# Attention and a soft mixture of experts: TensorE's flips of x, logits and slot sums stand in the rounds that complete a query tile

## The chip, the core and the metric

The kernel runs on one core of a Trainium2 chip. The metric is the device time of one execution in microseconds (us), the median of several. The profile comes from one execution, taken by the hardware profiler. Its engines are TensorE (PE; PEld is its weight load), VectorE (DVE), ScalarE (ACT), GpSimd (POOL) and SyncE (SP), which issues nearly all transfers.

## The reference

```
scores = scale * q @ k^T                      # 8 batches, 8 heads, 576 x 576, head size 64
scores = where(0 <= i - j < 128, scores - slope_h * (i - j), -1e9)
attn   = softmax(scores) @ v
x      = attn, heads side by side: 4608 tokens x 512
logits = x @ phi                              # 32 slots: 8 experts x 4
d = softmax of logits over the 4608 tokens    # per slot
slot_input = d^T @ x
slot_out   = relu(slot_input @ w1[e]) @ w2[e] # per expert, hidden size 1024
c = softmax of logits over the 32 slots       # per token
out = c @ slot_out
```

## The kernel before

A query tile (b, t) is 128 queries of batch b (t = 0 to 3), or the last 64 (t = 4). It is done in groups (b, t, g) of four heads by 128 queries: two groups for t below 4, one for t = 4, 72 in all. The window of 128 keys lets a group look at its own tile's keys and those of the tile before.

The loop over `groups` (L777) emits one round for each group, and the order in which it emits is the order in which each engine runs, since the schedule is written out by hand (`manual_schedule`). Semaphores are set from what each step reads and writes, and a PSUM bank counts as one thing: two engines never use one bank at once. In round i:

- VectorE runs `softmax_front`: `merge` of group i (L286, puts masked keys right), `rowmax` (L300), `inverse` of group i-1 (L313), `bias` (L304), `normalise` of group i-1 (L317). Between them stand single steps of the slot softmax (`filler`).
- TensorE flips the probabilities of group i-3 (`flip`, L374), ScalarE copies the flip out (`split`, L380), and GpSimd makes from it the part that lies in the own tile and the part in the tile before (two selects, L386 and L388).
- TensorE runs `values` of group i-4 (L410): v times the probabilities, into the only buffer `xp`. Where that completes a tile, VectorE copies it into `x` (`x_store`, L424), and the next `values` waits for that copy.
- TensorE runs the scores of group i+1 (`scores`, L261 the bias, L270 the products), into one of two buffers, which the exponentials of group i-1 must have left.
- ScalarE runs the exponentials of group i (`expo`, L359).
- Last, TensorE's extra steps of that round run (`run("pe", i)`), and VectorE's (`run("dve", i)`). ScalarE's extra steps stand behind `split`, VectorE's of the kind "pre" at the head of the round.

For the rounds up to 6 the flip and `values` are one group further on, and round 7 (`SKIP`) has none of them.

The extra steps are those of the mixture. Tiles are gathered into passes of four (the eighth has three, the last two), each tile of a pass in a lane. `after_values` puts down, for each completed tile, in which round its steps run: `x_flip` (L438, TensorE, into the same two banks as the flip of the probabilities), and `x_keep` a round later (L447, ScalarE, into `xns`). For each completed pass it puts down a chain: `logits` (L456, TensorE, reads the four tiles in `xts`), `token_copy` (L464, ScalarE), `token_max` (L469, VectorE), `slot_flip` (L477, TensorE), `token_exp` (L484), `token_sum` (L496, VectorE), `token_flip` (L502, TensorE), `token_keep` (L507, ScalarE), `slots_max` (L536 and L537, VectorE), `slot_sum` (L514, TensorE, reads `xns`), `slots_exp` (L540), `slot_add` (L522, VectorE, scales and adds to `acc`), and `slots_norm` in three single steps (L547 to L549). `logits`, the flips and the slot sum all use one PSUM bank (tag "mi"), one after the other. `turn` and `ready` keep the order: an `x_flip` of a pass comes no earlier than the slot sum of the pass before, and no two are in one round.

`x_store` of a tile of pass k+1 overwrites the lane of `xts` (`x_of`, L416) in which the tile of pass k stood; the short tiles (t = 4) have a buffer of their own.

The transfers of q, k, v and the experts' weights are issued by SyncE in the order of emission, each when its buffer is free. After the rounds come the last pass, the slot inputs, the experts' two products and the output; that part is long and fully written out.

Of the kernel before, what the change touches and what calls it, by code (L numbers as in the profile page):

```python
# [44 lines left out]
LAG = 4  # L45
SKIP = 7
# [26 lines left out]
def tile_attn_softmoe(  # L73
# [60 lines left out]
    def load_weight():  # L134
        n = loaded[0]
        loaded[0] += 1
        m, e, k = units[n]
        if NW <= n < NW + len(place):
            wt[units[n]] = place[n - NW]
        else:  # L140
            wt[units[n]] = wpool.tile([P, UW], F32, tag="w", name=f"w{n}")
        nc.sync.dma_start(wt[units[n]], (w1d, w2d)[m][e, :, UW * k:UW * (k + 1)])
# [4 lines left out]
    def order(b):  # L147
        return (1, 2, 3, 4, 0) if b == last else range(NT)

    def pos(b, t):  # L150
        return order(b).index(t)
# [4 lines left out]
    end = len(passes) - 1  # L156
# [5 lines left out]
    groups = [(b, t, g) for b in range(B) for t in order(b) for g in range(2 if t < 4 else 1)]  # L162
    number = {key: i for i, key in enumerate(groups)}
    n = len(groups)
# [22 lines left out]
    def load_v(again=False):  # L187
        if again:
            b, t, v_slot[last, 0] = last, 0, area[:, 13]
        else:  # L190
            b, t = v_loads[len(v_taken)]
            v_slot[b, t] = vs[len(v_taken) % 3]
            v_taken.append((b, t))
        nc.sync.dma_start(v_slot[b, t][0:width(t)], vd[b, P * t:P * t + width(t)])

    def load_v_pair():
        new = [len(v_taken), len(v_taken) + 1]
        for i in new:
            v_slot[v_loads[i]] = vs[i % 3]
            v_taken.append(v_loads[i])  # L200
        for o in (0, DM // 2):
            for i in new:
                b, t = v_loads[i]
                nc.sync.dma_start(
                    v_slot[b, t][:, o:o + DM // 2], vd[b, P * t:P * t + P, o:o + DM // 2])
# [210 lines left out]
    def x_of(b, t):  # L416
        return xts[lane(b, t)] if t < 4 else xt_t

    def x_store(b, t, eng=None, js=slice(0, NPAIR)):
        src = st[b, t][:, js]  # L420
        o, w = (0, P) if t < 4 else (TAIL * (b % 2), TAIL)
        dst = x_of(b, t)[:, js, o:o + w]
        if eng is None:
            nc.vector.tensor_copy(dst, src[:, :, 0:w])  # L424
        else:
            eng.copy(dst, src[:, :, 0:w])
# [22 lines left out]
    def lanes(k):  # L449
        return len(passes[k])  # L450
# [253 lines left out]
    todo = {}  # L704

    def do(when, i, fn, *a):
        todo.setdefault((when, i), []).append((fn, a))
# [18 lines left out]
    def load_weights_at(i):  # L726
# [5 lines left out]
        if b == last and (t == 0 and g == 0 or t == 4):  # L732
            assert loaded[0] >= NW
            load_weight()

    def after_values(i, key):
        b, t, g = key
        if not (g == 1 or t == 4):
            return
        p = pos(b, t)  # L740
        if (b, p) == (last - 1, NT - 1):
            load_v_pair()
        elif b + p and len(v_taken) < len(v_loads):
            load_v()
        x_store(b, t)
        if (b, t) not in pass_of:
            return
        k, c = pass_of[b, t]
        turn[0] = max(i + 1, turn[0] + 1, ready.get(k - 1, 0) + 4)
        do("pe", turn[0], x_flip, b, t)  # L750
        if (b, t) != tiles[-1]:
            do("act", turn[0] + 1, x_keep, b, t)
        if c == lanes(k) - 1:
            ready[k] = i
            do("pe", i + 1, logits, k)
            if k == end:
                return
            assert turn[0] <= i + 3
            do("act", i + 2, token_copy, k)
            do("dve", i + 2, token_max, k)  # L760
            do("pe", i + 2, slot_flip, k)
            do("act", i + 3, token_exp, k)
            do("dve", i + 3, token_sum, k)
            do("pe", i + 3, token_flip, k)
            do("act", i + 4, token_keep, k)
            do("pre", i + 4, slots_max, k)
            do("pe", i + 4, slot_sum, k)
            do("act", i + 5, slots_exp, k)
            do("dve", i + 5, slot_add, k)
            do("dve", i + 6, later, slots_norm, k)  # L770

    turn, ready = [0], {}

    with tc.manual_schedule(engines=ORDERED):
        scores(0)
        loads(0)
        for i in range(n):  # L777
            new = groups[i]
            run("pre", i)
            if i:  # L780
                softmax_front(new, groups[i - 1])
            else:
                for us in (LO, HI):
                    merge(new, us)
                    rowmax(new, us)
                    bias(new, us)
                    expo(new, us)
            near = int(i < SKIP)
            if i + near >= FLAG and i != SKIP:
                flip(groups[i + near - FLAG])  # L790
                split(groups[i + near - FLAG])
            run("act", i)
            if i + near >= LAG and i != SKIP:
                values(groups[i + near - LAG])
                after_values(i, groups[i + near - LAG])
            if i + 1 < n:
                scores(i + 1)
            if i + 1 < n - 1:
                loads(i + 1)
            if i:  # L800
                expo(new)
            run("pe", i)
            load_weights_at(i)
            run("dve", i)
# [324 lines left out]
```

## Time and profile before

| | |
|---|---|
| median of 3 runs | 286.34 us (286.32 to 286.56) |
| the profiled execution | 286.09 us |
| its span | 284.3 us |
| mean granted TensorE clock | 0.992 |
| rounds | from about 5 to 212 us |
| transfers | 72.49 MB, mean 255 GB/s |

The busy times of the five engines over the span, the busy times of single stretches, the waits (who waited for whom: total, times, longest), the chain of work that ended last, and the timeline (start, duration, engine, line, operation) are the views that the text uses. A line such as `PE xp L410 <- DVE area L424` reads: TensorE, about to run line 410 that writes `xp`, stood idle until VectorE's line 424, which writes `area`, was done. `area` is one large tile in which `x`, the probabilities, v and their flips all lie.

### The profile page before, as it was taken

To read this page: it belongs to the slowest core of one execution; us is meant where nothing else is said; L and a number is where in the kernel's file an instruction comes from. 1 tells how busy PE (TensorE), PEld (TensorE's weight loads), DVE (VectorE), ACT (ScalarE), POOL (GpSimd) and SP (SyncE) were. 2 spreads that over 40 slices of the span, in tenths; PEclk is the share of its full clock that TensorE was granted. 3 is DMA by queue.
4 is the path that set the end of the run, shared out by engine and by line. 5 is a ranking of instruction groups with operands and counts; after the bars stand their busy time and mean duration, and the time that the engine had idled before them with its cause. 6 is when DMAs were issued, how large, how long until landed. Compare 5 with 4: busy or idle time off the path is not lost.

```text
span 284.3 us, 11675 instructions
## 1 busy us (share of the span) xinstructions
PE 257.5 (91%) x4575; PEld 180.7 (64%) x4575; DVE 218.6 (77%) x546; ACT 190.5 (67%) x780; POOL 111.7 (39%) x221
## 2 busy tenths in 40 slices
PE   7789898989899999998989998998989899999990
PEld 3567676767577677676667766766666443587750
DVE  1789998997998898899999899897973352656352
ACT  2868868887798887897897888887774411044460
POOL 3035734481574385265527526556452011000000
PEclk9999999999999999999999999999999999999996
DMA  5735368889786998889698778876565588999997
GB/s 167 238 110 153 115 173 250 255 247 295 252 277 184 303 303 262 257 265 285 221 298 283 255 236 280 268 212 218 166 213 199 172 257 296 417 416 373 376 357 295
DMA packets 36767, 72.49 MB, mean 255 GB/s; under 512 B 4413, under 2 KB 15337, under 8 KB 36713
## 3 DMA queue, kind: packets, MB, share of 16 engines
q1 hardware_dynamic: 35992, 71.25, 75.7%
q8 instruction: 36, 0.59, 0.8%
q10 hardware_dynamic: 720, 0.51, 0.6%
q14 instruction: 19, 0.15, 0.2%
HBM read 62.30 MB, written 9.44 MB: 252 GB/s over the span
## 4 chain that ended last, share of the span: by engine, by line
PE 44%; DVE 38%; ACT 9%; issue 3%; DMA 3%; POOL 1%; DVEq 0%; ACTq 0%; SPq 0%; POOLq 0%
DVE area L317 12%; DVE s L300 9%; PE xp L410 8%; ACT area L359 6%; PE op L967 5%; PE s L270 5%; DVE area L424 5%; PE hp L930 5%; DVE s L286 4%; PE po L992 4%; PE s L261 2%; PE lp L456 2%; PE pq L374 2%; DVE acc L522 2%; DMA area<-v_n 2%
## 5 line engine op out<-in xcount | busy, mean ns | idle before, releaser
L359 ACT ACTIVATE area<-s,nb 128x128 f32<-128x128 f32 x286 | 101.9, 379 | 21.6 <-DVE nb L304 20.2
L410 PE MATMUL xp<-area 128*64 128x128 f32 (+1 forms) x1104 | 71.7, 270 | 9.5 <-DVE area L424 6.6
L410 PEld LDWEIGHTS xp<-area 128*64 128x64 f32 x1104 | 54.5, 137 | 16.4 <-POOL area L388 5.0
L359 ACT ACTIVATION_READ_ACCUMULATOR area<-s,nb 128x1 f32 x286 | 62.2, 218 | 0.0
L317 DVE TENSOR_TENSOR area<-area,rs 128x512 f32<-128x512 f32 (+1 forms) x73 | 59.9, 821 | 1.7 <-ACT area L447 0.4
L270 PE MATMUL s<-kq 64*64 64x192 f32 (+2 forms) x1144 | 57.0, 316 | 0.0
L386 POOL TENSOR_SCALAR_AFFINE_SELECT area<-area 128x512 f32<-128x512 f32 (+1 forms) x57 | 42.7, 748 | 26.9 <-ACT area L380 26.3
L380 ACT COPY area<-pq 128x512 f32<-128x512 f32 (+1 forms) x72 | 42.5, 592 | 16.0 <-PE pq L374 14.3
L300 DVE TENSOR_REDUCE s<-s 128x4 f32<-128x512 f32 (+1 forms) x72 | 50.0, 694 | 2.2
L388 POOL TENSOR_SCALAR_AFFINE_SELECT area<-area 128x512 f32<-128x512 f32 (+1 forms) x57 | 46.5, 817 | 3.9
L270 PEld LDWEIGHTS s<-kq 64*64 64x64 f32 x1144 | 41.2, 139 | 3.4
L309 POOL TENSOR_SCALAR rs<-sm 128x4 f32<-128x4 f32 x70 | 13.5, 193 | 71.2 <-ACT area L359 69.8
L286 DVE COPY_PREDICATED s<-cst,s 128x256 f32<-128x256 int32 (+1 forms) x72 | 30.2, 419 | 4.8 <-PE s L270 4.4
L374 PE MATMUL pq<-unit_r,area 64*128 64x64 f32 x552 | 31.4, 234 | 1.9 <-ACT area L322 1.2
L374 PEld LDWEIGHTS pq<-unit_r,area 64*128 64x128 f32 x552 | 23.0, 140 | 11.6 <-issue 5.0
L261 PE MATMUL s<-ramp,pair_of 64*64 64x384 bf16 x286 | 27.0, 358 | 2.5 <-ACT area L359 2.0
L424 DVE COPY area<-xp 128x512 f32<-128x512 f32 (+1 forms) x38 | 24.1, 633 | 3.6 <-PE xp L410 3.4
L447 ACT COPY area<-pq 128x512 f32<-128x512 f32 x34 | 20.2, 594 | 0.3 <-PE pq L432 0.3
L261 PEld LDWEIGHTS <-pair_of 64*64 64x64 bf16 x288 | 9.5, 106 | 15.7 <-issue 12.0
L438 PEld LDWEIGHTS pq<-unit_r,area 64*128 64x128 f32 x264 | 10.7, 138 | 13.2 <-issue 11.7
L994 ACT COPY ob<-po 128x512 f32<-128x512 f32 x19 | 10.4, 592 | 11.4 <-PE po L992 11.4
L994 DVE COPY ob<-po 128x512 f32<-128x512 f32 x17 | 11.2, 686 | 6.6 <-PE po L992 4.4
(164 smaller groups left out, 276.6 us busy)
## 6 DMA issues: line engine op xcount, KB each, us to landing
w<-w SPq DMA_DIRECT2D x53, 512.0 KB, 5.4
out<-ob SPq DMA_DIRECT2D x36, 256.0 KB, 3.6
kq<-q_t SPq DMA_DIRECT2D x69, 128.0 KB, 3.3
kq<-k_t SPq DMA_DIRECT2D x32, 256.0 KB, 3.4
area<-v_n SPq DMA_DIRECT2D x31, 256.0 KB, 4.5
area<-w SPq DMA_DIRECT2D x8, 512.0 KB, 4.9
area<-v_n SPq DMA_DIRECT2D x12, 128.0 KB, 5.2
kq<-w SPq DMA_DIRECT2D x3, 512.0 KB, 5.6
```

The lines of the kernel that those rows point to most:

```text
L261: nc.tensor.matmul(dst[strip], lhsT=pair_of[rows, int(t == 0), strip], rhs=src, start=True, stop=False)
L270: nc.tensor.matmul(parts[par][KB * jj:KB * jj + KB, second * u + KB * skip:second * u + WIN], lhsT=qt[rows, jj if t < 4 else j, KB * h:KB ...
L286: nc.vector.copy_predicated(to, keep, of)
L300: nc.vector.tensor_reduce(st[key]["mx"], merged(key, us), axis=AX.X, op=ALU.max, negate=True)
L317: nc.vector.tensor_tensor(p4, p4, bc(rs, 2, P), op=ALU.mult)
L359: nc.scalar.activation(s["p4"][:, u], src, AF.Exp, bias=s["nb"][:, u:u + 1], scale=SCALE, accum_out=s["sm"][:, u:u + 1],)
L374: nc.tensor.transpose(s["pt"][:, 2 * (u % 2) + u // 2, r], s["p4"][rows, u], ident[rows, rows])
L380: nc.scalar.copy(pa[:, us].rearrange("p u (r w) -> p u r w", r=2), s["pt"][:, us])
L386: nc.gpsimd.affine_select(prev, own, [[-step, m], [0, 4], [-1, KB]], ALU.is_gt, 0.0, base=-i0, channel_multiplier=1)
L388: nc.gpsimd.affine_select(own, own, [[step, m], [0, 4], [1, KB]], ALU.is_ge, 0.0, base=i0, channel_multiplier=-1)
L410: nc.tensor.matmul(xp[D * par:D * par + D, j, 0:w], lhsT=v_slot[b, t - 1 + ph][:, D * h:D * h + D], rhs=src[:, :, par, i] if t < 4 else sr ...
L424: nc.vector.tensor_copy(dst, src[:, :, 0:w])
```

## The change

The function `full_round(i)` gives the first round from i on whose `values` complete a tile (not round 7). `x_flip` is put into such a round instead of the next free one. So is `logits`. The chain behind `logits` keeps its steps, each one round behind the last, but the slot sum, too, waits for a round that completes a tile (except in the last two passes), and `ready` is now the slot sum's round. `slot_add` comes one round behind the slot sum. `x_store` is no longer emitted right behind `values` but at the head of VectorE's extra steps of the same round, so behind TensorE's extra steps; on VectorE it stands where it stood.

```diff
+    def of_round(i):
+        return groups[i + int(i < SKIP) - LAG]
+
+    def full_round(i):
+        for r in range(i, n):
+            if r != SKIP and of_round(r)[1:] in ((0, 1), (1, 1), (2, 1), (3, 1), (4, 0)):
+                return r
+        return i
+
     def after_values(i, key):
...
-        x_store(b, t)
+        todo.setdefault(("dve", i), []).insert(0, (x_store, (b, t)))
         if (b, t) not in pass_of:
             return
         k, c = pass_of[b, t]
-        turn[0] = max(i + 1, turn[0] + 1, ready.get(k - 1, 0) + 4)
+        turn[0] = full_round(max(i + 1, turn[0] + 1, ready.get(k - 1, 0)))
         do("pe", turn[0], x_flip, b, t)
         if (b, t) != tiles[-1]:
             do("act", turn[0] + 1, x_keep, b, t)
         if c == lanes(k) - 1:
-            ready[k] = i
-            do("pe", i + 1, logits, k)
+            first = full_round(i + 1)
+            do("pe", first, logits, k)
             if k == end:
                 return
-            assert turn[0] <= i + 3
-            do("act", i + 2, token_copy, k)
-            do("dve", i + 2, token_max, k)
-            do("pe", i + 2, slot_flip, k)
-            do("act", i + 3, token_exp, k)
-            do("dve", i + 3, token_sum, k)
-            do("pe", i + 3, token_flip, k)
-            do("act", i + 4, token_keep, k)
-            do("pre", i + 4, slots_max, k)
-            do("pe", i + 4, slot_sum, k)
-            do("act", i + 5, slots_exp, k)
-            do("dve", i + 5, slot_add, k)
-            do("dve", i + 6, later, slots_norm, k)
+            ready[k] = full_round(first + 3) if k < end - 1 else first + 3
+            assert turn[0] < ready[k]
+            do("act", first + 1, token_copy, k)
+            do("dve", first + 1, token_max, k)
+            do("pe", first + 1, slot_flip, k)
+            do("act", first + 2, token_exp, k)
+            do("dve", first + 2, token_sum, k)
+            do("pe", first + 2, token_flip, k)
+            do("act", first + 3, token_keep, k)
+            do("pre", first + 3, slots_max, k)
+            do("pe", ready[k], slot_sum, k)
+            do("act", first + 4, slots_exp, k)
+            do("dve", ready[k] + 1, slot_add, k)
+            do("dve", first + 5, later, slots_norm, k)
```

## The prediction

> **What bounds the kernel now.** I read the page's busy shares first, then the busy times of the rounds' stretch (12 to 208 us), then the waits of that stretch, and last the timeline of one pass. The page:
>
> ```profile
> PE 257.5 (91%) x4575; PEld 180.7 (64%) x4575; DVE 218.6 (77%) x546; ACT 190.5 (67%) x780; POOL 111.7 (39%) x221
> ```
>
> The 77% of DVE is an average over two stages. The diff touches only the rounds, so I asked for their stretch up to the stall at 193 us, and for who waited for whom between 12 and 208 us (total, times, longest):
>
> ```profile
> 12.00:193.00 181.00, 169.88 (x3305) 124.07 (x3305) 165.29 (x403) 148.64 (x648) 93.52 (x175) 1.00 0.76 240
> ...
> PE xp L410 <- DVE area L424: 6.6, 11, 1.0
> ...
> PE s L261 <- ACT area L359: 2.0, 3, 0.8
> ...
> DVE area L424 <- PE xp L410: 3.4, 5, 0.8
> ```
>
> In these 181 us TensorE is busy for 169.88 (94%) and VectorE for 165.29 (91%). Neither alone is the bound: they hand the end of the chain to each other. Eleven times TensorE's `values` (L410) waits for `x_store` (L424) to empty the one bank it writes, 6.6 us in all; five times `x_store` waits for `values`, 3.4 us. The granted clock is 1.00, so no time lies there. The next rows are one pass end, rounds 36 to 43 (start, duration, engine, line; the bracket is the wait before it):
>
> ```profile
> 107.25 1.15 DVE L317 TENSOR_TENSOR area<-area,rs 128x512 f32<-128x512 f32 x1
> 108.32 0.68 DVE L424 COPY area<-xp 128x512 f32<-128x512 f32 x1
> 109.14 1.09 PE L410 MATMUL xp<-area 128*64 128x128 f32 x16 [0.70 <-DVE area L424]
> 110.17 0.36 PE L261 MATMUL s<-ramp,pair_of 64*64 64x384 bf16 x4
> 111.10 0.46 PE L438 MATMUL pq<-unit_r,area 64*128 64x64 f32 x8
> 111.50 1.08 PE L456 MATMUL lp<-area,phi 128*32 128x128 f32 x32
> 112.51 0.46 PE L374 MATMUL pq<-unit_r,area 64*128 64x64 f32 x8
> 112.60 0.69 DVE L317 TENSOR_TENSOR area<-area,rs 128x512 f32<-128x512 f32 x1
> 112.89 1.10 PE L410 MATMUL xp<-area 128*64 128x128 f32 x16
> 113.92 0.36 PE L261 MATMUL s<-ramp,pair_of 64*64 64x384 bf16 x4
> 114.04 0.69 DVE L424 COPY area<-xp 128x512 f32<-128x512 f32 x1 [0.75 <-PE xp L410]
> 114.65 0.28 DVE L469 TENSOR_REDUCE nm<-lg 128x1 f32<-128x129 f32 x1
> 115.00 0.43 DVE L286 COPY_PREDICATED s<-cst,s 128x256 f32<-128x256 int32 x1
> ...
> 115.51 1.15 PE L410 MATMUL xp<-area 128*64 128x64 f32 x32
> 116.35 0.69 DVE L317 TENSOR_TENSOR area<-area,rs 128x512 f32<-128x512 f32 x1
> 116.59 0.36 PE L261 MATMUL s<-ramp,pair_of 64*64 64x384 bf16 x4
> 116.96 0.42 DVE L424 COPY area<-xp 128x256 f32<-128x256 f32 x1
> 117.29 0.21 DVE L496 SCALAR_TENSOR_TENSOR fine<-fine,al,sb 128x1 f32<-128x1 f32 x1
> 117.53 0.33 PE L502 MATMUL dp<-unit_r,lg 128*128 128x128 f32 x1
> 117.78 0.46 PE L374 MATMUL pq<-unit_r,area 64*128 64x64 f32 x8
> 117.89 0.29 DVE L536 TENSOR_REDUCE cm<-dp 128x4 f32<-128x128 f32 x1 [0.39 <-PE dp L502]
> 118.43 0.42 DVE L286 COPY_PREDICATED s<-cst,s 128x256 f32<-128x256 int32 x1
> 118.77 0.36 PE L261 MATMUL s<-ramp,pair_of 64*64 64x384 bf16 x4
> 119.70 1.07 PE L514 MATMUL ap<-area,dn 128*32 128x512 f32 x8
> 120.36 0.42 DVE L286 COPY_PREDICATED s<-cst,s 128x256 f32<-128x256 int32 x1
> 120.70 0.46 PE L438 MATMUL pq<-unit_r,area 64*128 64x64 f32 x8
> 121.00 0.41 PE L374 MATMUL pq<-unit_r,area 64*128 64x64 f32 x8
> ...
> 121.93 0.36 PE L261 MATMUL s<-ramp,pair_of 64*64 64x384 bf16 x4
> 122.57 0.68 DVE L424 COPY area<-xp 128x512 f32<-128x512 f32 x1
> 123.17 0.74 DVE L522 SCALAR_TENSOR_TENSOR acc<-acc,al,ap 128x512 f32<-128x512 f32 x1
> ...
> 124.54 0.36 PE L261 MATMUL s<-ramp,pair_of 64*64 64x384 bf16 x4
> 125.85 0.42 DVE L286 COPY_PREDICATED s<-cst,s 128x256 f32<-128x256 int32 x1
> ```
>
> Two regimes stand here. Up to 109 us VectorE ends last: `normalise` (L317) runs into `x_store`, and TensorE waits 0.70 us for it. From 110 to 118 us TensorE ends last: scores, `x_flip` (L438) and `logits` (L456) stand ahead of the next `values`, and `x_store` waits 0.75 us for those.
>
> **What the change moves.** No instruction is added or removed; TensorE steps change their round. I worked the rounds out from the two versions of `after_values`. An `x_flip` now stands in a round whose `values` complete a tile, ahead of the next round's flip and `values`. `logits` stays in rounds 12, 21, 66 and 71 and goes one round later in passes 2 to 6 (to 29, 38, 45, 54, 61). `slot_sum` of passes 0 to 6 goes one round later, of pass 6 two (63 to 65). Their ScalarE copies and VectorE steps go with them. SyncE's queue is passed by nothing: every load keeps its place in it. GpSimd keeps its order too, but for `m_run`'s small step, which goes with `token_exp`.
>
> *Price of the moved flip.* From its start to the start of the flip behind it: 120.70 to 121.00, 0.30 us of TensorE. Behind each of the eleven waits stands, in the new order, an `x_flip` just ahead of the waiting `values` (before 109.14 it is x_flip(3,1), which was behind the scores of round 35). A wait is 6.6/11 = 0.60 us on average, so at most 11 x 0.30 = 3.3 us of TensorE's work goes under them. What hides it is `normalise` plus `x_store`; if these were quicker it would cost its 0.30 again. The gain counts only where TensorE ends last in the rounds after. In the quoted piece that is so from 110 us on, but there the second effect bites.
>
> *A wait that is added.* `x_store` of the first tile of a pass writes the lane of `xts` that `logits` of the pass before reads. In the old order `logits` was a round earlier. In the new one both are in the same round in passes 3 to 6 (rounds 38, 45, 54, 61), and the diff puts `x_store` behind TensorE's part, so it must wait for `logits`. Behind it on VectorE stand `merge`, `rowmax` and `bias` of the next round (so ScalarE's exponentials), and TensorE's next `values`. In pass 2 the tile before is a short one with another buffer, so no such wait.
>
> *The walk of pass 3*, with start-to-start steps from the rows. TensorE: scores(38) stays at 110.17; nothing follows, so the flip is at 111.10, `values` +0.38 at 111.48, scores(39) +1.03 at 112.51 (before: 113.92). Then x_flip(3,2) +0.93, logits +0.40 at 113.84, done +1.01 at 114.85. VectorE: `normalise` ends at 113.29 as before and `x_store` waits 1.56 us instead of 0.75, to 114.85; `merge`(39) +0.61 (114.04 to 114.65) at 115.46, 0.46 later than before and with `token_max` (114.65 to 115.00, 0.35) still owed: 0.8 behind. TensorE waits for that `x_store` (115.54, and 0.14 as from 109.00 to 109.14) until 115.68; before 115.51.
> It is then won back. TensorE: scores(40) +1.08 at 116.76; scores(41) as far on as before (2.18, with a slot flip for a token flip) at 118.94, before 118.77. VectorE: 115.46 + 1.35 (115.00 to 116.35) + 0.61 (to 116.96) + 0.33 (to 117.29) and `token_max`'s 0.35 makes `merge`(40) 118.10, before 118.43; owed are now token sum (0.21) and the two slot steps (0.54), and the wait of 0.39 at 117.89 is gone. The step to the next `merge` is 1.93 (118.43 to 120.36); with the owed 0.75, `merge`(41) is at 120.78, and `x_store`(4,0) 1.35 + 0.61 later at 122.74, before 122.57. From there on the work is the same with slot_add elsewhere in it (3.28, 122.57 to 125.85): `merge`(43) at 126.02, before 125.85. TensorE again: scores(42) came 3.16 after scores(41); without slot sum and x_flip (119.70 to 121.00, 1.30) but with a token flip (117.53 to 117.78, 0.25) it is 2.11, so 121.05. Then 0.93, slot sum and x_flip 1.30, flip 0.38: `values` at 123.66, and scores(43) +1.03 at 124.69, before 124.54.
>
> So 0.1 to 0.2 late, with only x_flip(3,4) owed, and that goes under the next wait for `x_store`. Price: 0.15 us for each of four passes, +0.6. Its bounds: 0, and 0.8 each if nothing is won back.
>
> *The other passes.* Pass 2 has one of the five waits of `x_store` for `values` (3.4/5 = 0.7 each); it goes without a new wait, but slot sum and a flip (1.30) come later in TensorE's row: I take -0.2, between 0 and -0.7. Three times the scores wait for ScalarE's exponentials, 2.0 us in all; two of these are in the first rounds, where an x_keep now leaves the exponentials' way: -0.2, between 0 and -0.7. Passes 0 and 1 keep their rounds but for slot sum: 0.
>
> *The end of the rounds* hangs on a transfer, as the chain in order of time and TensorE's timeline show:
>
> ```profile
> 192.69 0.47 PE xp L410 x8
> ...
> 193.17 4.58 DMA area<-v_n
> ...
> 197.89 0.66 PE L410 MATMUL xp<-area 128*64 128x128 f32 x8 [0.73 <-DMA area<-v_n]
> ```
>
> Whatever happens before it is worth what it does to the `values` at 192.69. There x_flip(6,2) leaves TensorE's way (-0.30) and slot_add of pass 6 VectorE's (-0.74 at most, by 123.17), while slot sum and x_flip(6,1) now stand right ahead of it; I take -0.2, with -0.7 and +0.3 as ends. `logits` of pass 7 (round 66) now waits for slot_add of pass 6 to empty its bank, since that add is now in the same round: at most 0.74 us, under the 0.73 of the transfer; without that cover it would cost 0.74. Nothing of the diff runs after the rounds.
>
> Sum: +0.6 - 0.2 - 0.2 - 0.2 = 0. The profiled execution took 286.09 us (span 284.3 and 1.8 around it); it stays at 286.1, and the median of the runs shown, 286.34, at 286.3. About 0.2%, 0.57 us, is what can be told from no change here.
>
> **The rivals.** *A, TensorE sets the pace throughout.* For it: 94% busy against 91%. Then the 3.3 us under the waits are all gained, less about 0.45 us of TensorE idle (115.23 to 115.68) at each of four new waits, 1.8: -1.5, 284.8 us. Against it: the eleven waits themselves, behind a busy VectorE.
>
> *B, the added wait isn't won back.* Place: rounds 38, 45, 54, 61; price 0.8 each, 3.2 us, 289.5 us. It decides if VectorE finds no idle time to shed in the four rounds behind, as it did at 117.89. For it: VectorE's row is nearly closed from 118 to 126. Partly so, it gives 287 to 288.
>
> *C, the selects fall on the normalise.* With `logits` gone from ahead of it, the flip of rounds 29, 38, 45, 54, 61 comes 1.4 us earlier (112.51 to 111.10), and so do GpSimd's two selects. `normalise` took 0.69 at 112.60, 1.15 at 107.25. Five times 0.46 is 2.3 us at most; four of the five are under the added wait, so I take half the rest and echoes, 1.4: 287.7 us.
> The Trainium skill (SBUF — State Buffer, Who interferes with whom) says that a VectorE instruction with two SBUF inputs and a GpSimd instruction that reads SBUF exclude each other, the later one blocking until the first has finished. By it the long `normalise` is one that met a running select; the two rows agree in size, and which select was running they don't show.
>
> *D, nothing is moved that anyone waits for* gives no change, the same time as the forecast.
>
> **How the numbers follow.** The forecast, with D: 0.40. A: 0.32. B: 0.18. C: 0.10. Faster by over 0.2%: 0.32 (A); within: 0.40; slower: 0.28 (B and C). The forecast's own range is 285.8 to 286.9. The range for 8 in 10 goes from 284.8 (A's full gain) to 287.9 (C and a part of B), leaving out B at its full price.
>
> **What would show it.** Right: the total of `values` waiting for `x_store` falls from 6.6 us to about 4; `x_store` waits on L456 four times, 0.7 to 1.6 us each; the wait on the transfer stays; the merge(43) stands within 0.3 us of 125.85. Wrong: waits on L456 with VectorE late four rounds on (B), more `normalise` of 1.15 than of 0.69 right behind the moved flips (C), or a merge(43) over 0.5 us early (A). A wait by `logits` of pass 7 that outlasts the transfer would also break the sum.

## The result and the profile after

| | before | after |
|---|---|---|
| median, same chip, 6 runs each | 286.11 us (285.79 to 286.56) | 289.65 us (289.20 to 291.63) |
| ratio | | 1.0132 (1.0103 to 1.0162) |
| the profiled execution, its span | 286.09, 284.3 us | 289.2, 287.5 us |

The change costs 1.3%, some 3.5 to 3.8 us. The forecast was no change, and the time lies above the range. Here and below a ratio leaves disturbed executions out, a median does not. TensorE's clock is not what changed: the granted clock of the stretches from 30 to 212 us is 1.00 before and after, and only from 12 to 30 us it is lower (0.91 after, 1.00 before), where after is ahead.

The page of after, the busy shares and the costliest groups (busy time, mean ns of one, idle time before them and what ended it):

```profile
PE 258.4 (90%) x4575; PEld 181.0 (63%) x4575; DVE 220.5 (77%) x546; ACT 192.5 (67%) x780; POOL 114.2 (40%) x221
...
L317 DVE TENSOR_TENSOR area<-area,rs 128x512 f32<-128x512 f32 (+1 forms) x73 | 63.5, 870 | 1.7 <-ACT area L447 0.4
L388 POOL TENSOR_SCALAR_AFFINE_SELECT area<-area 128x512 f32<-128x512 f32 (+1 forms) x57 | 50.3, 882 | 3.9
...
L424 DVE COPY area<-xp 128x512 f32<-128x512 f32 (+1 forms) x38 | 24.0, 631 | 5.2 <-PE lp L456 4.9
```

The same two groups on the page of before:

```profile
L317 DVE TENSOR_TENSOR area<-area,rs 128x512 f32<-128x512 f32 (+1 forms) x73 | 59.9, 821 | 1.7 <-ACT area L447 0.4
L388 POOL TENSOR_SCALAR_AFFINE_SELECT area<-area 128x512 f32<-128x512 f32 (+1 forms) x57 | 46.5, 817 | 3.9
```

Two things are new. The 73 `normalise` (L317) have the same shapes and take 3.6 us more; the second select (L388) takes 3.8 us more. And `x_store` (L424) now stands idle for `logits` (L456). The waits of after between 12 and 212 us (total, times, longest):

```profile
PE xp L410 <- DVE area L424: 7.3, 13, 1.2
...
DVE area L424 <- PE lp L456: 4.9, 4, 1.5
...
DVE area L424 <- PE xp L410: 0.4, 1, 0.4
```

The wait of `values` for `x_store` did not fall from 6.6 us, it rose to 7.3. The five waits of `x_store` for `values` (3.4 us) became four for `logits` (4.9 us). The end of pass 3 in TensorE's timeline of after:

```profile
112.33 1.10 PE L410 MATMUL xp<-area 128*64 128x128 f32 x16
113.35 0.36 PE L261 MATMUL s<-ramp,pair_of 64*64 64x384 bf16 x4
...
114.29 0.46 PE L438 MATMUL pq<-unit_r,area 64*128 64x64 f32 x8
114.68 1.08 PE L456 MATMUL lp<-area,phi 128*32 128x128 f32 x32
115.69 0.46 PE L374 MATMUL pq<-unit_r,area 64*128 64x64 f32 x8
116.62 1.15 PE L410 MATMUL xp<-area 128*64 128x64 f32 x32 [0.47 <-DVE area L424]
```

and in VectorE's:

```profile
112.09 0.43 DVE L286 COPY_PREDICATED s<-cst,s 128x256 f32<-128x256 int32 x1 [0.31 <-PE s L270]
...
115.78 0.69 DVE L424 COPY area<-xp 128x512 f32<-128x512 f32 x1 [1.34 <-PE lp L456]
116.39 0.42 DVE L286 COPY_PREDICATED s<-cst,s 128x256 f32<-128x256 int32 x1
...
127.25 0.41 DVE L286 COPY_PREDICATED s<-cst,s 128x256 f32<-128x256 int32 x1
```

The order is the one that the prediction walked through: scores, flip of x, `logits`, `x_store`, and then a `values` that waits 0.47 us for it. `merge` of group 39 stands at 116.39 (115.00 before), that of group 43 at 127.25 (125.85 before). But after was late already at `merge` of group 38, before any added wait: 112.09 against 111.25.

So I followed the lag, the start of the same `merge` in after less that in before. The rows of groups 12, 34, 45 and 71 in VectorE's timeline of before:

```profile
38.03 0.41 DVE L286 COPY_PREDICATED s<-cst,s 128x256 f32<-128x256 int32 x1
...
100.87 0.42 DVE L286 COPY_PREDICATED s<-cst,s 128x256 f32<-128x256 int32 x1
...
131.54 0.42 DVE L286 COPY_PREDICATED s<-cst,s 128x256 f32<-128x256 int32 x1
...
208.59 0.42 DVE L286 COPY_PREDICATED s<-cst,s 128x256 f32<-128x256 int32 x1
```

and of after:

```profile
36.81 0.41 DVE L286 COPY_PREDICATED s<-cst,s 128x256 f32<-128x256 int32 x1
...
101.58 0.41 DVE L286 COPY_PREDICATED s<-cst,s 128x256 f32<-128x256 int32 x1
...
132.04 0.41 DVE L286 COPY_PREDICATED s<-cst,s 128x256 f32<-128x256 int32 x1
...
211.75 0.42 DVE L286 COPY_PREDICATED s<-cst,s 128x256 f32<-128x256 int32 x1
```

The third row is how much longer the `normalise` up to that point took in after than in before, summed over VectorE's timeline of both:

| group of the `merge` | 12 | 34 | 38 | 39 | 45 | 54 | 56 | 71 |
|---|---|---|---|---|---|---|---|---|
| lag, us | -1.22 | +0.71 | +0.84 | +1.39 | +0.50 | +2.64 | +1.98 | +3.16 |
| `normalise`, summed, us | -0.82 | +1.22 | +0.84 | +1.16 | +1.01 | +1.64 | +2.08 | +3.24 |

Single columns swing, because steps have moved from one round to another: the lag is +0.43 at group 40 and +1.35 at group 41.

The change first gains 1.2 us. Between groups 12 and 34 it loses 1.9 us, and in the same stretch its `normalise` take 2.0 us longer. The first added wait comes only after that, in round 38.

### The profile page after: what moved, and what is told of

Read it like the earlier page. It is cut to its first block, busy times and chain, and to the rows that moved or that the text cites. A ratio compares the mean times of both kernels' runs of the same rounds, so it can differ in the third digit from the quotient of the medians.

```text
span 287.5 us, 11660 instructions
## 1 busy us (share of the span) xinstructions
PE 258.4 (90%) x4575; PEld 181.0 (63%) x4575; DVE 220.5 (77%) x546; ACT 192.5 (67%) x780; POOL 114.2 (40%) x221
## 4 chain that ended last, share of the span: by engine, by line
PE 48%; DVE 33%; ACT 9%; POOL 3%; issue 3%; DMA 1%; DVEq 0%; ACTq 0%; SPq 0%
DVE area L317 10%; PE xp L410 9%; DVE s L300 7%; PE s L270 6%; DVE area L424 5%; PE op L977 5%; ACT area L359 5%; PE hp L940 5%; DVE s L286 4%; PE po L1002 4%; PE s L261 3%; PE lp L456 3%; PE pq L374 3%; PE pq L438 2%; POOL area L386 2%
## 5 line engine op out<-in xcount | busy, mean ns | idle before, releaser
L317 DVE TENSOR_TENSOR area<-area,rs 128x512 f32<-128x512 f32 (+1 forms) x73 | 63.5, 870 | 1.7 <-ACT area L447 0.4
L359 ACT ACTIVATION_READ_ACCUMULATOR area<-s,nb 128x1 f32 x286 | 59.7, 209 | 0.0
L388 POOL TENSOR_SCALAR_AFFINE_SELECT area<-area 128x512 f32<-128x512 f32 (+1 forms) x57 | 50.3, 882 | 3.9
L386 POOL TENSOR_SCALAR_AFFINE_SELECT area<-area 128x512 f32<-128x512 f32 (+1 forms) x57 | 41.3, 725 | 24.9 <-ACT area L380 23.9
L424 DVE COPY area<-xp 128x512 f32<-128x512 f32 (+1 forms) x38 | 24.0, 631 | 5.2 <-PE lp L456 4.9
L438 PEld LDWEIGHTS pq<-unit_r,area 64*128 64x128 f32 x264 | 10.7, 137 | 12.6 <-issue 12.1
```

What stands on the lines that cost most here:

```text
L317: nc.vector.tensor_tensor(p4, p4, bc(rs, 2, P), op=ALU.mult)
L359: nc.scalar.activation(s["p4"][:, u], src, AF.Exp, bias=s["nb"][:, u:u + 1], scale=SCALE, accum_out=s["sm"][:, u:u + 1],)
L386: nc.gpsimd.affine_select(prev, own, [[-step, m], [0, 4], [-1, KB]], ALU.is_gt, 0.0, base=-i0, channel_multiplier=1)
L388: nc.gpsimd.affine_select(own, own, [[step, m], [0, 4], [1, KB]], ALU.is_ge, 0.0, base=i0, channel_multiplier=-1)
```

## The experiments

Two theories stood: the added wait of `x_store` is not won back (theory S below, the prediction's rival B), and `normalise` and the selects of GpSimd fall on each other (theory C, its rival C). The ratios are against the kernel before, run beside them on the same chip.

**A buffer of its own.** After, but the first tile of every other pass goes to a separate buffer, so that no `x_store` overwrites what `logits` of the same round reads. `xt_0` lies in the tile of `lg`, behind the columns that the rounds use, widened by 128; to make room, a tile of the part behind the rounds (`dn`) is narrowed.

```diff
     def x_of(b, t):
+        if (b, t) in pass_of and lane(b, t) == 0 and pass_of[b, t][0] % 2 and t < 4:
+            return xt_0
         return xts[lane(b, t)] if t < 4 else xt_t
```

> The changed kernel, but the first tile of every second pass has a buffer of its own, so x_store never writes what logits of the same round reads. Theory S (the added wait: x_store stands idle 4.9 us for logits, four times, and the four rounds behind can't win it back): the wait on L456 goes, and with it nearly all of the loss: 285.5 to 286.8 us. Theory C (contention: the new positions of the flips bring GpSimd's selects under the normalise more often, whose 73 instructions took 63.5 us instead of 59.9): the wait goes, but normalise stays above 62 us in sum and the time at 288 to 289.5 us.

Measured: 288.33 us, ratio 1.0068 (1.0042 to 1.0094). Lines were added above, so L288 is `merge`, L319 `normalise` and L428 `x_store`. The row of `normalise` on its page:

```profile
L319 DVE TENSOR_TENSOR area<-area,rs 128x512 f32<-128x512 f32 (+1 forms) x73 | 61.4, 841 | 1.7 <-ACT area L451 0.4
```

and its VectorE timeline:

```profile
36.58 0.41 DVE L288 COPY_PREDICATED s<-cst,s 128x256 f32<-128x256 int32 x1
...
101.37 0.41 DVE L288 COPY_PREDICATED s<-cst,s 128x256 f32<-128x256 int32 x1
...
111.88 0.43 DVE L288 COPY_PREDICATED s<-cst,s 128x256 f32<-128x256 int32 x1 [0.31 <-PE s L272]
...
114.17 0.68 DVE L428 COPY area<-xp 128x512 f32<-128x512 f32 x1
114.77 0.41 DVE L288 COPY_PREDICATED s<-cst,s 128x256 f32<-128x256 int32 x1
...
131.32 0.42 DVE L288 COPY_PREDICATED s<-cst,s 128x256 f32<-128x256 int32 x1
...
209.28 0.42 DVE L288 COPY_PREDICATED s<-cst,s 128x256 f32<-128x256 int32 x1
```

The wait on `logits` is gone, the time is the one that theory C named, but `normalise` is at 61.4 us, below its 62: with the wait 2.1 us (63.5 - 61.4) of longer `normalise` went too. Against after this kernel is 0.21 us ahead at group 38 (112.09 - 111.88). At group 39, behind the first added wait, it is 1.62 ahead (116.39 - 114.77), at group 45 0.72 (132.04 - 131.32), at group 71 2.47 (211.75 - 209.28). So an added wait costs 1.4 us where it stands, and within six rounds 0.9 of that is won back; what stays is (2.47 - 0.21)/4 = 0.57 us per wait in these two executions, and 0.64% by the ratios, 1.8 us in all or 0.46 each. The wait, with the longer `normalise` that went with it, explains about half of the loss. The other half is in this kernel too: from group 12 to 34 it goes from 1.45 us ahead of before (38.03 - 36.58) to 0.50 behind (101.37 - 100.87), with no wait on `logits`.

**The flips of x alone.** After, with `logits` and slot sum where before has them.

```diff
-            first = full_round(i + 1)
+            first = i + 1
...
-            ready[k] = full_round(first + 3) if k < end - 1 else first + 3
+            ready[k] = first + 3
```

A last line keeps the flip of a pass's last tile within three rounds (`turn[0] = min(turn[0], i + 3)`).

> Only x_flip goes to the rounds that complete a tile; logits and slot sum keep the rounds of before, so there is no wait of x_store for logits. Theory S: not slower than before, 285.0 to 286.4 us. Theory C: normalise above 61.5 us in sum, 287 to 289 us.

Measured: 286.62 us, ratio 1.0011 (0.9992 to 1.0031), no change, 0.2 us above theory S's range. `values` waits for `x_store` 6.4 us in 13 places: ten are places of before's eleven, where the waits come to 4.9 us now, and three are new, with 1.5 us. So part of the flips did go under the old waits, and the time did not fall. Its page:

```profile
L317 DVE TENSOR_TENSOR area<-area,rs 128x512 f32<-128x512 f32 (+1 forms) x73 | 59.4, 814 | 1.5 <-DVE nb L304 0.4
```

`normalise` is as in before (59.9). The flips by themselves neither gain nor lose.

**Logits and slot sum alone.** After, with `x_flip` in the next free round.

```diff
-        turn[0] = full_round(max(i + 1, turn[0] + 1, ready.get(k - 1, 0)))
+        turn[0] = max(i + 1, turn[0] + 1, ready.get(k - 1, 0))
```

> The other half: logits and slot sum in the rounds that complete a tile, x_flip in the next free round as before. The four waits of x_store for logits are there. Theory S: 288.5 to 290 us, as slow as the whole change. Theory C: normalise near 60 us in sum and at most 1.5 us slower than before, 286 to 287.6 us.

Measured: 288.01 us, ratio 1.0071 (1.0045 to 1.0096), between the two theories' ranges. Its page:

```profile
L317 DVE TENSOR_TENSOR area<-area,rs 128x512 f32<-128x512 f32 (+1 forms) x73 | 62.6, 858 | 1.7 <-ACT area L447 0.4
...
L424 DVE COPY area<-xp 128x512 f32<-128x512 f32 (+1 forms) x38 | 24.0, 633 | 4.5 <-PE lp L456 4.0
```

Both symptoms come with the chain, not with the flips: `normalise` 62.6 us, the added wait 4.0 us. Half of the loss is here; the other half needs both parts of the change together.

**The slot sum early.** After, with `logits` late but the slot sum three rounds behind it.

```diff
-            ready[k] = full_round(first + 3) if k < end - 1 else first + 3
+            ready[k] = first + 3
```

> The changed kernel with only the slot sum back three rounds behind logits, whatever that round completes. Theory S: as slow as the changed kernel, 289.2 to 290 us. Theory C gives no size; a normalise sum nearer to 60 us should go with a time nearer to 286, by about as many us as the sum falls.

Measured: 289.37 us, ratio 1.0119 (1.0087 to 1.0150), as after within the intervals. The edit moves three slot sums, from rounds 16, 25 and 65 to 15, 24 and 64. `normalise` falls to 62.4 us, the waits on `logits` stay at 4.9. By the `merge` of group 30 this kernel is 1.40 us ahead of after, 1.0 of it by shorter `normalise` in rounds 16, 17 and 25, and the lead is still 1.52 at group 67 (198.96 - 197.44). A round later it is gone. Groups 67 and 68, and the `values` between them, in the timelines of this kernel:

```profile
197.44 0.41 DVE L286 COPY_PREDICATED s<-cst,s 128x256 f32<-128x256 int32 x1
...
201.06 0.66 PE L410 MATMUL xp<-area 128*64 128x128 f32 x8 [1.45 <-DMA area<-v_n]
...
202.73 0.43 DVE L286 COPY_PREDICATED s<-cst,s 128x256 f32<-128x256 int32 x1 [2.05 <-PE s L270]
```

and of after:

```profile
198.96 0.42 DVE L286 COPY_PREDICATED s<-cst,s 128x256 f32<-128x256 int32 x1
...
202.70 0.43 DVE L286 COPY_PREDICATED s<-cst,s 128x256 f32<-128x256 int32 x1 [0.37 <-PE s L270]
```

So the slot sum's place is worth 1.4 us in the rounds of these two executions, and the transfer at their end takes that back: `values` waits for it 1.45 us here and not at all in after. The time is the one that theory S named, but not for its reason.

The same edit on the kernel with a buffer of its own:

> The changed kernel with the buffer of its own and the slot sum three rounds behind logits. In the traces so far the kernel with the early slot sum was 1.6 us ahead of before at round 29 and lost it in the passes with the added wait. Theory S: without that wait the lead holds, 284.3 to 285.8 us, the fastest so far. Theory C: it is given back to longer normalises, 286 to 287.5 us.

Measured: 287.21 us, ratio 1.0036 (1.0016 to 1.0057), slower than before still, but better than with either edit alone. Its page:

```profile
L319 DVE TENSOR_TENSOR area<-area,rs 128x512 f32<-128x512 f32 (+1 forms) x73 | 60.3, 826 | 1.3
```

With the added wait gone and `normalise` almost back at before's 59.9 us, most of the loss is gone; the time is the one that theory C named, but longer `normalise` are not its reason. In the profiled execution the last `merge` is only 0.18 us later than in before. The rest of the 1.2 us by which its span is longer (285.5 against 284.3) lies behind the rounds, a stretch that took 75.6 to 76.8 us from trace to trace. No version that was run with the selects beats before.

**No reading by GpSimd.** `normalise` multiplies probabilities by inverse sums, both in SBUF. In before and after its length varies between 0.69 and 1.15 us in the rows shown. One that began ahead of the select, in the timelines of before:

```profile
51.29 0.69 DVE L317 TENSOR_TENSOR area<-area,rs 128x512 f32<-128x512 f32 x1
51.84 0.67 POOL L386 TENSOR_SCALAR_AFFINE_SELECT area<-area 128x512 f32<-128x512 f32 x1 [0.86 <-ACT area L380]
```

The same `normalise`, that of round 16, in the timelines of after:

```profile
50.03 0.66 POOL L386 TENSOR_SCALAR_AFFINE_SELECT area<-area 128x512 f32<-128x512 f32 x1 [0.27 <-ACT area L380]
50.07 1.15 DVE L317 TENSOR_TENSOR area<-area,rs 128x512 f32<-128x512 f32 x1
50.75 0.99 POOL L388 TENSOR_SCALAR_AFFINE_SELECT area<-area 128x512 f32<-128x512 f32 x1
```

In before the `normalise` began first and took 0.69 us. There slot sum stood ahead of the flip, from 49.35 us on; in after it starts at 50.49, behind that flip, so the flip and its selects come earlier. In after the select began 0.04 us earlier, the `normalise` took 1.15, and the second select, begun while that ran, took 0.99 instead of 0.66.

The other `normalise` agree. Counted in the timelines, the 70 full-size ones by what GpSimd was doing when they began (number, length in us; the last column is a kernel of below, in which GpSimd writes instead of selecting):

| GpSimd was running | before | after | before's order, three writes |
|---|---|---|---|
| a select, or a write | 35, mean 0.96 | 44, mean 0.98 | 47, 0.69 |
| its product in `slots_norm` (L549; L548 with the writes), which reads two tiles | 6, 0.71 to 0.87 | 7, 0.86 to 0.87 | 6, 0.71 to 0.86 |
| nothing | 29, 0.69 | 19, 0.69 | 17, 0.69 |

Where more than 0.2 us of a select was left, the `normalise` took what was left plus 0.53 us (0.22 left gave 0.76, 0.66 left gave 1.19); two of before that began within 0.01 us of a select took 0.69, and that select 1.2. After has nine more that began under a select.

To test it, both selects of a group were replaced by writes of a constant into the same places; `values` then multiplies v by a constant, so the masking into own and previous tile is left out, and every instruction keeps its place in its engine's order.

```diff
-            nc.gpsimd.affine_select(
-                prev, own, [[-step, m], [0, 4], [-1, KB]], ALU.is_gt, 0.0, base=-i0, channel_multiplier=1)
-            nc.gpsimd.affine_select(
-                own, own, [[step, m], [0, 4], [1, KB]], ALU.is_ge, 0.0, base=i0, channel_multiplier=-1)
+            nc.gpsimd.memset(prev, 0.01)
+            nc.gpsimd.memset(own, 0.01)
```

The order of before, of after, and of after with a buffer of its own:

> The kernel before, with GpSimd's two selects of a group replaced by two memsets of the same tiles (0.01 in all places, so the values use that and not the probabilities): same order, same number of GpSimd instructions, same waits, but GpSimd only writes. By the Trainium skill (SBUF — State Buffer, Who interferes with whom) a VectorE instruction with two SBUF inputs is blocked by a GpSimd instruction that reads SBUF, not by one that only writes. If so, normalise is at 0.69 us in nearly all of its 70 full-size instructions (sum about 49 us instead of 59.9) and the kernel several us faster, 277 to 284. If the long normalise has another cause, its sum stays at 59 to 61 and the time near 286.

> The changed kernel with the same memsets in place of the selects. Against the same of the kernel before: Theory C (contention) says the difference all but goes: within 0.8 us. Theory S (the added wait) says that it stays: 2 to 3.5 us slower. Both at work: 1 to 2 us slower.

> The changed kernel with the buffer of its own for the first tile and with the memsets: neither the added wait nor contention. If these two are the whole loss it is no slower than the kernel before with memsets, and by the 11 waits of values for x_store up to 2 us faster. If it is still slower by over 0.6 us, a third cause is left, such as the later slot sums.

Measured: before's order 281.16 us, ratio 0.9789 (0.9748 to 0.9830); after's 280.95 us, 0.9821 (0.9790 to 0.9851); the buffer of its own 279.01 us, 0.9748 (0.9719 to 0.9777). The page of after's order:

```profile
L317 DVE TENSOR_TENSOR area<-area,rs 128x512 f32<-128x512 f32 (+1 forms) x73 | 50.9, 698 | 1.6 <-ACT area L380 0.4
```

The long ones are gone, `normalise` falls by 12.6 us (63.5 to 50.9), and the time by 2 to 3%. The intervals of before's and after's order overlap, so this does not yet tell the theories apart. But two writes of 0.52 us are also shorter than two selects. So the three kernels were run again with three writes per group (the part in the tile before is written twice), 1.55 us against the selects' (42.7 + 46.5)/57 = 1.57 us in before:

```diff
+            nc.gpsimd.memset(prev, 0.02)
             nc.gpsimd.memset(prev, 0.01)
             nc.gpsimd.memset(own, 0.01)
```

> The order of before; both GpSimd selects are replaced by three memsets (the own part gets one, the part in the tile before two), so values multiply v with a constant. Three memsets of 0.518 us are 1.55 us of GpSimd per group, about what the two selects took (0.75 + 0.82 = 1.57 us), but they read nothing. Theory (the reading of SBUF beside the normalise is the cost): normalise stays at 0.69 us on average and the time stays within 1 us of the two-memset kernel's 281.2 us. Rival (that kernel was quicker because GpSimd was done 0.5 us earlier in each group): the time returns to 284 us or more although normalise stays short.

> The order of after with the same three memsets in place of the two selects. Theory (of the 3.7 us that the change costs, about half is the added wait and the other half longer normalises): normalise 0.70 us, the added waits of x_store on logits stay at 5 to 6 us, and the time is 1 to 2 us above this order's own-buffer version of the same job and at most 1.5 us above the order of before without selects. Rival (the whole cost is order alone): 3 us or more above the order of before without selects.

> The order of after with a buffer of its own for the first tile of every other pass (no wait of x_store on logits) and the three memsets. Theory: with neither the added wait nor the contention the change costs nothing or gains up to 1.5 us against the order of before with three memsets. Rival (something else in the order costs too): 1 us or more slower than it.

Measured: 280.54 us, ratio 0.9824 (0.9799 to 0.9849); 282.26 us, 0.9883 (0.9861 to 0.9906); 280.98 us, 0.9833 (0.9807 to 0.9859). The page of before's order with three writes:

```profile
L317 DVE TENSOR_TENSOR area<-area,rs 128x512 f32<-128x512 f32 (+1 forms) x73 | 50.1, 687 | 1.8 <-DVE nb L304 0.4
...
L388 POOL MEMSET area<- 128x512 f32 (+1 forms) x57 | 29.5, 518 | 3.2 <-ACT area L380 2.9
L387 POOL MEMSET area<- 128x512 f32 (+1 forms) x57 | 29.5, 517 | 3.3
```

and from the waits of after's order (between 12 and 212 us; L423 is `x_store`, L455 `logits`):

```profile
DVE area L423 <- PE lp L455: 6.1, 4, 1.8
```

GpSimd is occupied as long as with selects. The waits are not the same, though the expectation took them to be: the first write needs nothing of ScalarE's copy (`split`), and GpSimd's waits for that copy fall from 26.3 us in 42 places to 2.9 in 4. But the last write ends 1.41 us behind the copy (median), and a pair of selects that no `normalise` held up ends 1.46 behind it (15 of 55 in before; the others 1.80). Two writes end at 0.83, and before's order stays at 280.5 us with three: its gain comes in the main from what GpSimd doesn't read, not from its being done sooner.

With the contention gone, the change costs 282.26 - 280.54 = 1.7 us instead of 3.5 to 3.8 (at most 1.5 was expected), and with the wait gone too, 280.98 - 280.54 = 0.4 us, whose intervals overlap. So about 1.3 us is the added wait (282.26 - 280.98; 1.8 with selects), and of the own-buffer order's 0.68%, 1.9 us, some 1.5 was contention; by the intervals each of these sizes can be off by about 1 us. GpSimd's length is not without effect in after's order: with three writes instead of two it took 282.26 us instead of 280.95, and with its own buffer 280.98 instead of 279.01.

## Why the prediction was wrong

**The steps that held.** That VectorE hands the end of the chain to TensorE and back fits the runs: where its `normalise` are short, every order is 1.2 to 2.5% faster than before. The added wait came where it was said, four times, 0.79 to 1.52 us (0.7 to 1.6 forecast), and each time the next `values` waited 0.46 to 0.47 us for the late `x_store`. In pass 3 the walk itself came close: `merge` of group 39 lost 1.39 - 0.84 = 0.55 us against the one before it (forecast 0.46), and up to group 45 that was won back against before. The sign that the prediction named, a `merge` of group 43 within 0.3 us of 125.85, failed: it stands at 127.25, and 0.84 us of that lag was there before the pass.

**"It is then won back ... Price: 0.15 us for each of four passes."** This step failed. One pass was walked and taken for all four. In it the later `logits` helps as much as the wait costs: with its own buffer group 39 is 0.23 us ahead of before although group 38 was 0.63 behind. In the next pass it does not: from group 45 to 56 the lag grows by 1.48 us (0.50 to 1.98), and with the own buffer by 0.18. The wait's own price is the difference to the order without it: 1.4 us at its place and 0.46 to 0.57 left of it, so 1.8 us for four and not 0.6. That is under the named bound of 0.8 each; the value was taken from the lower end. It is rival B at half price.

**"C ... 0.10", 1.4 us.** The forecast's sum had no term for this at all, and the rival's size was too small and in the wrong place. C looked for selects that come earlier because `logits` had left the place ahead of the flip, in rounds 29 to 61. The first loss came in round 16, where slot sum left that place, and in groups 12 to 34, where no added wait stands, 2.0 us of longer `normalise` went with 1.9 us of lag. In all `normalise` took 3.6 us more, 2.1 of them only together with the added wait. Taking GpSimd's reads away takes about 2 us off what the change costs (3.5 to 3.8 against 1.7), and 1.5 us in the own-buffer order (1.9 - 0.4). The Trainium skill (SBUF — State Buffer, Who interferes with whom) says that a VectorE instruction with two SBUF inputs and a GpSimd instruction that reads SBUF shut each other out, whichever begins first going through. The runs agree: 0.69 us where the `normalise` began first, 1.15 where the select was 0.04 us ahead, and 0.69 in all 47 that began under a write. The prediction had weighed it as a rival of 1 in 10. It belongs in the sum here, since the moved steps of TensorE changed when the flips and so the selects start.

**"At most 3.3 us goes under the waits ... to about 4."** Failed: 7.3 us, and 6.4 in the kernel that moves the flips alone. In after 5.4 of the 7.3 us stand in nine of before's eleven places, each behind a moved flip, and 1.9 us behind the four added waits. Four of the nine became shorter by 0.2 to 0.6 us, as forecast. But four grew, those at 57.76 and 83.83 us most, from 0.75 and 0.64 to 1.09 and 1.15; with the slot sum early these two are 0.50 each. And with the flips alone the shorter waits were no gain in time.

**The first rounds and pass 2, -0.2 each.** The first rounds were undersized: `merge` of group 12 is 1.22 us earlier, of which 0.82 is shorter `normalise`. It did not last, so it tells little of the sum. Pass 2 went the other way: from group 29 to 36 the lag grew by 0.67 us, with 0.70 of longer `normalise`.

**The end of the rounds.** "The wait on the transfer stays" failed: TensorE's timeline of after has none.

```profile
196.53 1.15 PE L410 MATMUL xp<-area 128*64 128x64 f32 x32
...
199.19 1.07 PE L456 MATMUL lp<-area,phi 128*32 128x128 f32 x24 [0.18 <-DVE acc L522]
...
200.59 1.09 PE L410 MATMUL xp<-area 128*64 128x128 f32 x16
```

The `values` that before began at 192.69 is 3.84 us late at 196.53; the one behind the transfer is in one piece and without its 0.73 us of waiting. `logits` of pass 7 does wait for `slot_add`, 0.18 us, within the 0.74 that were named. The `values` come late enough to find the transfer done, so 0.73 of the 3.84 us is given back there, and no more. The same transfer took the lead of the kernel with the early slot sum.

Rival A, 0.32, found no support: the moved flips alone gain nothing (1.0011). The chances failed in one more way: B and C were priced as alternatives, 0.18 and 0.10, and both came: 1.8 us for the wait and 1.5 for the contention that is left without it, and 0.4 of the order that the intervals don't settle. How much belongs to which depends on what is taken away first: without reads the wait costs 1.3 us.

**What stays open.** Why the wait brings 2.1 us of longer `normalise` with it was not isolated. Of the 1.2 us by which the spans of the two own-buffer kernels are longer than before's, only 0.69 us (slot sum late) and 0.18 us (early) are there at the last `merge`; whether the rest, behind the rounds, is chance or comes of the narrowed `dn` is open. Why the slot sum late needs the moved flips for its full cost (0.71% without them, 1.32% with) was seen and not explained.

## What to carry to other kernels

A step moved on one engine changes when the engines behind it start, and so which instructions of VectorE and GpSimd meet: before a reordering, list the VectorE instructions with two SBUF inputs, and count how many begin under a running GpSimd instruction that reads. An emission order that is moved also makes new write-after-read waits (here the lane of a four-lane buffer); price such a wait against the order without it as well as against the old one, and at more than one of its places. Room under a wait is a gain only if the engine that is waited for stops ending last.

## What the runs showed of the hardware

Two figures were not expected. The length of `normalise` falls from 0.82 to 0.69 us on average when GpSimd writes its two tiles without reading, in all 70 full-size cases no longer than 0.87 us, where it reached 1.19 us with selects; taking those reads away is worth 1.8 to 2.1% of the time of before, more than the whole change cost. And it is a matter of when, not of how much GpSimd does: with the same selects, 35 of the 70 `normalise` began under one in before and 44 in after, where only steps of TensorE and what follows them had moved.
